# Strict load order, eight raw buffers and a held-back second half of batch 2, in a fused window-attention and mixture-of-experts kernel

The chip is one Trainium2, and the kernel runs on one of its cores. The metric is the device time of one execution in microseconds (us). Engines are named as in the profile: PE is TensorE (PEld its weight loads), DVE is VectorE, ACT is ScalarE, POOL is GpSimd, SP is SyncE. SPq, ACTq and POOLq are their instruction queues, where the issue of a DMA is recorded.

## The reference

```
B, H, S, D = 8, 8, 576, 64
scores = q @ k.T / sqrt(D), kept where |i - j| <= 32, softmax, then @ v
x      = heads side by side                            # (8, 576, 512)
e_idx  = argmax(x.mean(axis=1) @ w_gate)               # one expert per batch
out[b] = gate_w[b] * (relu(x[b] @ w1[e_idx[b]]) @ w2[e_idx[b]])
```

Each batch needs 2.36 MB of q and k in four loads, 1.18 MB of v, and 2.1 MB of fp16 weights of an expert that is known only when its attention is done. Each batch writes 1.18 MB in five stores.

## The kernel before

A small scheduler (the "plan") writes every operation into the in-order queues of the engines at build time. Three parts matter here. The plan gives each load a priority and a buffer:

```
buffers("raw", [P, 2, J, D], FP32, 5)        # q, k as loaded; batch 0 borrows weight space
vraws = buffers("vraw", ..., 2)
...
other = b == 1 and quad == 0                 # two loads of batch 1 go out by ScalarE
plan.add("ACT" if other else "SP", 0.6, f"ld{name}{b}{quad}", load,
         deps=["CT00k12_"] if other else [],
         takes=[("raw", 1)] if b else [], land=580e3, prio=-100 if other else base + quad)
```

A v load is a small tail (8 KB, first) and a bulk of 1.18 MB in rows of 256 bytes. Both go out by SyncE. The weights go out by GpSimd once the gate knows the expert. The last part is the output: ScalarE scales a PSUM tile into `osb` and then issues its store itself, from the same in-order queue:

```
nc.scalar.activation(osb[:, 0:w], bank..., ACTF.Copy, scale=gwb)      # "evac"
...
nc.scalar.dma_start(out[b, 128 * i : 128 * i + 128, :], osb)          # "store"
```

The softmax here doesn't subtract the row's maximum and nothing guards it: scores larger than these inputs give would overflow.

Of the kernel before, what the change touches and what calls it, by code (L numbers as in the profile page):

```python
# [10 lines left out]
FP32 = mybir.dt.float32  # L11
# [9 lines left out]
D = 64  # L21
# [4 lines left out]
P = 128  # L26
# [3 lines left out]
J = S // G  # L30
# [188 lines left out]
def kernel(  # L219
# [10 lines left out]
    nc = tc.nc  # L230
# [4 lines left out]
    plan = Plan()  # L235

    def buffers(name, shape, dtype, n):
        tiles = [sb.tile(shape, dtype, name=f"{name}{i}") for i in range(n)]
        plan.resource(name, tiles)
        return tiles  # L240


    rowi = sb.tile([P, 32], FP32, name="rowi")
    buffers("raw", [P, 2, J, D], FP32, 5)
    vraws = buffers("vraw", [P, NVS + 1, D], FP32, 2)
    w1s = buffers("w1", [P, NDT, F], FP16, 2)
    w2s = buffers("w2", [P, NFT, DM], FP16, 2)
# [1 line left out]
    roomy = [  # L249
        t.rearrange("p a c -> p (a c)").bitcast(FP32)[:, 0 : 2 * J * D]  # L250
        .rearrange("p (h j d) -> p h j d", h=2, j=J)
        for t in (w1s[0], w2s[0], w1s[1], w2s[1])
    ]
# [37 lines left out]
    zero = sb.tile([P, P], FP16, name="zero")  # L291
# [62 lines left out]
    def warm(op):  # L354
# [4 lines left out]
             deps=[f"CT11{n}" for n in ("q12", "k12")], prio=500)  # L359
# [7 lines left out]
    raw = {}  # L367
# [20 lines left out]
    def add_batch(b):  # L388
        base = b * 1000


        for quad in range(2):
            for name, src in (("q", q), ("k", k)):
                def load(op, b=b, quad=quad, name=name, src=src):
                    t = op.got["raw"][0] if b else roomy.pop(0)
                    raw[(b, quad, name)] = t
                    (nc.scalar if op.eng == "ACT" else nc.sync).dma_start(
                        t.rearrange("p h j d -> p h (j d)"),
                        src[b, 4 * quad : 4 * quad + 4]
                        .rearrange("(h x) s d -> (x s d) h", h=2)  # L400
                        .rearrange("(p r) h -> p h r", p=P),
                    )
                other = b == 1 and quad == 0
                plan.add("ACT" if other else "SP", 0.6, f"ld{name}{b}{quad}", load,
                         deps=["CT00k12_"] if other else [],
                         takes=[("raw", 1)] if b else [],
                         land=580e3, prio=-100 if other else base + quad)

                for part, (j0, j1) in enumerate(PARTS):
                    def cast(op, b=b, quad=quad, name=name, part=part, j0=j0, j1=j1):  # L410
                        if part == 0:
                            qkb_of[(b, quad, name)] = op.got["qkb"][0]
                        dst = qkb_of[(b, quad, name)][:, j0:j1]
                        src = raw[(b, quad, name)].rearrange("p h j d -> p j h d")[:, j0:j1]
                        if op.eng == "SW":
                            nc.gpsimd.tensor_copy(dst, src)  # L416
                        else:
                            nc.scalar.copy(dst, src)
                    cn = f"c{name}{b}{quad}"
                    plan.add("SW/ACT" if b < 2 else "SW",  # L420
                             {"SW": 0.68, "ACT": 0.66} if part == 0 else {"SW": 0.55, "ACT": 0.56},
                             f"{cn}{part}", cast,
                             deps=[f"ld{name}{b}{quad}"] + ([f"{cn}0_"] if part else [])
                             + (["W10_"] if b == 2 else [])
                             + (["vr010_"] if b == 1 and quad else []),
                             takes=[] if part else [("qkb", 1)],
                             frees=[(f"ld{name}{b}{quad}", "raw")] if part and b else [],
                             prio=base + quad, port=0.6)

        for half in range(2):  # L430
            def loadv(op, half=half):

                if half == 0:
                    vr_of[b] = op.got["vraw"][0]
                    if b == 0:
                        va_of[b] = op.got["vaug"][0]
                t = vr_of[b]
                rows = v.rearrange("b h s d -> (b h s) d")
                r0 = b * H * S - 32
                if half:  # L440
                    j0 = 0 if b else 1
                    nc.sync.dma_start(
                        t[:, j0:NVS],
                        rows[r0 + 128 * j0 : r0 + 128 * NVS].rearrange("(j p) d -> p j d", p=P),
                    )
                    return
                if b == 0:
                    nc.sync.dma_start(t[32:P, 0], rows[0:96])
                nc.sync.dma_start(t[0:32, NVS], rows[r0 + 128 * NVS : r0 + 128 * NVS + 32])
            plan.add("SP", 0.6 if half or b else 1.0, f"ldv{b}{half}", loadv,  # L450
                     takes=[] if half else [("vraw", 1)] if b else [("vraw", 1), ("vaug", 1)],
                     land=1.4e6 if half else 0.03e6, prio=base + 2 + half,
                     deps=["zero"] + ([f"ldv{b}0_"] if half else []))

            def vcast(op, half=half):
                if half == 0 and b:
                    va_of[b] = op.got["vaug"][0]
                for j0, j1 in ((19, 28), (28, NVS + 1)) if half else ((0, 9), (9, 19)):
                    dst, src = va_of[b][:, 0, j0:j1, 0:D], vr_of[b][:, j0:j1]
                    if op.eng == "SW":  # L460
                        nc.gpsimd.tensor_copy(dst, src)  # L461
                    else:
                        copy(op, dst, src)
            plan.add(BOTH if b == 1 else "DVE" if b == 0 and not half else "SW",
                     {"DVE": 1.0, "ACT": 1.3, "SW": 1.25}, f"vc{b}{half}", vcast,
                     deps=[f"ldv{b}1", f"ldv{b}0"]
                     + (["cc"] if b == 0 else [f"S{b}000_"] if b > 1 else ["G0_"])
                     + (["vr000_", "vr001_"] if b == 0 and half else [])
                     + ([f"vc{b}0_"] if half else []),
                     takes=[] if half or b == 0 else [("vaug", 1)],  # L470
                     frees=[(f"ldv{b}0", "vraw")] if half else [],
                     prio=base + (2 + half if b == 0 else 120), port=0.6)

            for up in range(2):
                def rot(op, half=half, up=up):

                    s = slice(18 * half, 18 * half + 18)
                    t = slice(18 * half + up, 18 * half + 18 + up)
                    va = va_of[b]
                    if up:  # L480
                        copy(op, va[64:P, 1, s, 0:D],
                             va[0:64, 0, t, 0:D] if b or not half else vr_of[0][0:64, t])
                    else:
                        nc.vector.tensor_copy(va[0:64, 1, s, 0:D], va[64:P, 0, t, 0:D])  # L484
                plan.add("ACT" if b == 0 and up and half else "DVE", 1.15 if b == 0 and up and half else 0.5,
                         f"vr{b}{half}{up}", rot,
                         deps=["ldv01", "ldv00", "cc"] + ["XS0111"] * half if b == 0 and up and half else [f"vc{b}{half}"],
                         prio=base + (4 + half if b == 0 else 120), port=0.5)


        for quad in range(2):
            for name in ("q", "k"):
                for part, (j0, j1) in enumerate(PARTS):
# [3 lines left out]
                    def tr(op, quad=quad, name=name, j0=j0, j1=j1, first=first, tn=tn):  # L497
# [5 lines left out]
                        for j in range(j0, j1):  # L503
# [4 lines left out]
                             deps=[f"c{name}{b}{quad}{part}"] + ([f"T{b}{quad}{name}0"] if part else [])  # L508
                             + (["ca"] if b == 0 else []),
                             takes=[("psA" if b > 1 else "psE", 1)] + ([(name + "T", 1)] if first else []),  # L510
                             frees=[] if first else [(f"c{name}{b}{quad}0", "qkb")],
                             prio=base + (40 if b else 3) * quad + (10 if b else 1) * part)

                    def tcopy(op, quad=quad, name=name, j0=j0, j1=j1, tn=tn):
                        pv = bank_of[tn].bitcast(BF16).rearrange("p (j c) -> p c j", c=P)
                        dst = qkT[(b, quad, name)]
                        if name == "k":
# [8 lines left out]
                             deps=[tn] + (["G0_"] if b == 1 and quad else []),  # L526
                             frees=[(tn, "psA" if b > 1 else "psE")],
                             prio=base + (40 if b else 3) * quad + (10 if b else 1) * part)
# [3 lines left out]
        for n in range(5):  # L532
            half, quad = n // 2, n % 2
# [43 lines left out]
            if b == 0:  # L577
# [3 lines left out]
                     deps=[f"CT{b}{a}{x}{p}2" for x in "qk" for p in range(2) for a in quads]  # L581
# [3 lines left out]
                     takes=[("psA", 2)] + ([] if n else [("E", 1)]),  # L585
                     frees=[(f"T{b}{a}{x}0", x + "T") for a in range(2) for x in "qk"]
# [376 lines left out]
```

## Time and profile before

| | before |
|---|---|
| time, median of 3 runs (range) | 227.77 us (227.43 to 230.16) |
| profiled execution | span 228.3 us, PE busy 92%, mean clock 0.983 |
| PE's one long stop | 4.01 us, for batch 0's first weight |
| PE idle between 46 and 221 us | 4.85 us (175.00 less 170.15 busy) |

The 40 slices of the page show the whole run at a glance. Each digit is the busy share of a slice of 5.7 us, in tenths:

```profile
PE   7989992999998999999988999699999999999980
PEclk9999999799999999999999999999999999999996
DMA  6999999799999999999999899989932993798041
```

The 2 in the PE row is the stop at 35 to 39 us, and the 7 below it is the clock that fell behind it. The DMA engines are full until about 160 us.

A second reading turned out to matter far more than that stop. ScalarE's timeline around the second large stop shows the issue of a store (start us, us, engine, line, operation, count; in brackets the idle time before it and its releaser):

```profile
65.78 1.39 ACT L868 ACTIVATE hT<-bank 128x288 f16<-128x288 f32 x3 [0.80 <-PE bank L850]
69.27 0.35 ACTq L923 DMA_DIRECT2D out_dram<-osb  x1
69.66 1.01 ACT L868 ACTIVATE hT<-bank 128x288 f16<-128x288 f32 x3 [2.50 <-PE bank L504]
```

Nothing runs on ScalarE from 67.2 to 69.27. Then the store is issued, and the next activation follows at once. ScalarE had stood at the store. PE lost 0.75 us by it.

### The profile page before, as it was taken

How to read it: one execution, taken by the hardware profiler on the slowest of the kernel's cores; microseconds unless marked ns; L12 is line 12 of the kernel's file. 1: busy time of each engine (PE TensorE's matmuls, PEld its weight loads, DVE VectorE, ACT ScalarE, POOL GpSimd, SP SyncE). 2: the span in 40 equal slices, each digit the busy share in tenths (PEclk: the TensorE clock that was granted, in tenths of full speed). 3: DMA queues.
4: the chain of work that ended last, by engine and by line, in shares of the span. 5: the costliest groups of instructions: out<-in, count | busy, mean ns of one | idle time of the engine just before them, and what ended most of it. 6: DMA issues, size and time to landing. Idle time of an engine off the chain costs nothing. (4 is left out here: it accounts for less than half of the span.)

```text
span 228.3 us, 6814 instructions
## 1 busy us (share of the span) xinstructions
PE 209.8 (92%) x2778; PEld 155.4 (68%) x2778; DVE 144.5 (63%) x369; ACT 148.5 (65%) x332; POOL 80.0 (35%) x126
## 2 busy tenths in 40 slices
PE   7989992999998999999988999699999999999980
PEld 5757762896488756986587758685598568749630
DVE  6478784156986897959866878569987676000000
ACT  4667981569657972898338955599289647647540
POOL 6436190008961193059033920459104100200000
PEclk9999999799999999999999999999999999999996
DMA  6999999799999999999999899989932993798041
GB/s 223 352 395 288 303 311 229 174 387 301 237 286 399 287 176 249 350 347 230 245 374 304 192 234 325 294 236 197 231 119 26 205 230 120 121 213 230 15 170 37
DMA packets 26639, 55.03 MB, mean 241 GB/s; under 512 B 2064, under 2 KB 12272, under 8 KB 24560
## 3 DMA queue, kind: packets, MB, share of 16 engines
q0 software_dynamic: 2304, 16.78, 38.0%
q1 hardware_dynamic: 18112, 27.21, 35.2%
q10 hardware_dynamic: 6192, 10.62, 12.4%
q8 instruction: 21, 0.34, 0.6%
q14 instruction: 10, 0.08, 0.1%
HBM read 61.94 MB, written 9.44 MB: 313 GB/s over the span
## 5 line engine op out<-in xcount | busy, mean ns | idle before, releaser
L850 PE MATMUL bank<-xT,w 128*128 128x288 f16 x512 | 75.0, 292 | 7.4 <-DMA w<-in_moe_w_dram 4.0
L850 PEld LDWEIGHTS <-w 128*128 128x128 f16 x512 | 61.6, 146 | 9.9 <-DMA w<-in_moe_w_dram 4.3
L868 ACT ACTIVATE hT<-bank 128x288 f16<-128x288 f32 x128 | 50.7, 424 | 16.7 <-PE bank L850 11.4
L886 PE MATMUL bank<-w,hT 128*128 128x512 f16 x256 | 60.5, 380 | 0.0
L416 POOL CAST qkb<-raw 128x640 bf16<-128x640 f32 (+1 forms) x54 | 42.7, 833 | 27.2 <-DMA raw<-in_q_dram 16.5
L912 ACT ACTIVATE osb<-bank,gwb 128x512 f32<-128x512 f32 (+1 forms) x40 | 25.8, 645 | 37.0 <-PE bank L886 33.0
L599 ACT ACTIVATE E<-bank 128x512 f16<-128x512 f32 (+1 forms) x80 | 41.7, 585 | 2.9 <-PE bank L557 2.8
L886 PEld LDWEIGHTS <-hT 128*128 128x128 f16 x256 | 23.1, 98 | 23.8
L820 POOL DMA_DIRECT2D w<-in_moe_w_dram x8 | 5.0, 630 | 83.2 <-DVE gw L812 47.3
L617 DVE TENSOR_TENSOR E<-E,mask 128x1024 f16<-128x1024 f16 (+1 forms) x30 | 25.7, 876 | 7.7 <-ACT E L599 7.5
L651 DVE TENSOR_TENSOR xs<-bank,linv 128x256 f16<-128x256 f32 (+2 forms) x88 | 27.6, 348 | 1.8
L504 PE MATMUL bank<-id_bf,qkb 128*128 128x128 bf16 x288 | 23.3, 219 | 1.2 <-ACT xT L386 1.2
L504 PEld LDWEIGHTS <-qkb 128*128 128x128 bf16 x288 | 18.7, 98 | 4.8 <-issue 1.3
L461 POOL CAST vaug<-vraw 128x576 f16<-128x576 f32 (+1 forms) x26 | 19.8, 815 | 0.0
L633 PEld LDWEIGHTS <-E 128*64 128x64 f16 x640 | 12.5, 111 | 8.2 <-issue 6.1
L386 ACT COPY xT<-bank 128x512 f16<-128x512 f16 (+1 forms) x24 | 12.3, 540 | 8.0 <-DVE kT L384 2.8
L633 PE MATMUL bank<-vaug,E 128*64 128x65 f16 x640 | 15.5, 197 | 1.8 <-DVE vaug L384 1.2
L557 PEld LDWEIGHTS <-kT 64*128 64x128 bf16 x576 | 10.7, 95 | 9.3 <-issue 7.7
L355 PE MATMUL bank<-wide,zero 128*128 128x256 f16 x94 | 15.5, 303 | 1.4 <-POOL wide L297 1.4
L557 PE MATMUL bank<-qT,kT 64*128 64x64 bf16 x576 | 15.4, 191 | 0.0
L384 DVE COPY xT<-bank 128x512 f16<-128x512 f16 (+1 forms) x16 | 6.4, 403 | 13.9 <-PE bank L711 13.8
L643 DVE RECIPROCAL linv<-bank 128x7 f32<-128x7 f32 (+2 forms) x56 | 10.5, 188 | 6.0 <-PE bank L633 5.9
(71 smaller groups left out, 200.2 us busy)
## 6 DMA issues: line engine op xcount, KB each, us to landing
w<-in_moe_w_dram POOLq DMA_DIRECT2D x16, 1024.0 KB, 13.0
out_dram<-osb ACTq DMA_DIRECT2D x32, 256.0 KB, 6.0
raw<-in_q_dram SPq DMA_DIRECT2D x13, 576.0 KB, 12.3
raw<-in_k_dram SPq DMA_DIRECT2D x13, 576.0 KB, 14.1
w<-in_q_dram SPq DMA_DIRECT2D x2, 576.0 KB
w<-in_k_dram SPq DMA_DIRECT2D x2, 576.0 KB, 7.6
out_dram<-osb ACTq DMA_DIRECT2D x8, 128.0 KB
raw<-in_q_dram ACTq DMA_DIRECT2D x1, 576.0 KB, 6.3
```

The source lines that it names most:

```text
L416: nc.gpsimd.tensor_copy(dst, src)
L461: nc.gpsimd.tensor_copy(dst, src)
L504: nc.tensor.transpose(pv[:, j - j0, :], qkb_of[(b, quad, name)][:, j], id_bf)
L557: nc.tensor.matmul(bank[:, 64 * place : 64 * place + 64], qkT[(b, a, "k")][rows, k0 : k0 + P], qkT[(b, a, "q")][rows, k0 : k0 + 64], start ...
L599: nc.scalar.activation(dst, src, ACTF.Exp, bias=0.0, scale=0.125)
L617: nc.vector.tensor_tensor(ev, ev, mv, ALU.mult)
L633: nc.tensor.matmul(bank[64 * n : 64 * n + 64, 65 * u : 65 * u + 65], E_of[b][:, h, 64 * block : 64 * block + 64], va_of[b][:, late, slot, ...
L651: nc.vector.tensor_tensor(xv[:, quad, hp : hp + u1 - u0], hv[0:n, u0:u1, 0:64], linv[0:n, u0:u1].to_broadcast([n, u1 - u0, 64]), ALU.mult,)
L850: nc.tensor.matmul(bank[:, 0:288], w_of[b][0].rearrange("p t (c n) -> p t n c", c=P)[:, dt, ft], xT_of[b][:, dt, 288 * c : 288 * c + 288], ...
L868: nc.scalar.activation(h_of[(b, ft)][:, 288 * c : 288 * c + 288], bank_of.pop(gn)[:, 0:288], ACTF.Relu,)
L886: nc.tensor.matmul(bank, h_of[(b, ft)][:, 128 * i : 128 * i + 128], w2s[:, ft, :], start=(ft == 0), stop=(ft == NFT - 1),)
L912: nc.scalar.activation(osb[:, 0:w], bank_of.pop(f"2{b}{i}")[:, 0:w], ACTF.Copy, bias=0.0, scale=tiny("gwb", [P, 1], FP32, b),)
```

## The change

The intent is to get batch 0's first weight sooner. The loads follow one strict order from SyncE alone. Eight raw buffers replace five, so that a load need not wait for a buffer. Batch 2's second q and k, its v and everything behind them wait for a one-column GpSimd write that stands behind the issue of batch 0's weights.

```
-    buffers("raw", [P, 2, J, D], FP32, 5)
+    buffers("raw", [P, 2, J, D], FP32, 8)
...
+                held = (b, quad, name) == (2, 1, "q")
+                def hold(op, b=b, quad=quad, name=name):
+                    t = raw[(b, quad, name)] = op.got["raw"][0]
+                    nc.gpsimd.memset(t[:, 0, 0, 0:1], 0.0)
+                if held:
+                    plan.add("SW", 0.1, "hold", hold, deps=["W20_"], takes=[("raw", 1)], prio=-5)
...
-                    (nc.scalar if op.eng == "ACT" else nc.sync).dma_start(
+                    nc.sync.dma_start(
...
-                other = b == 1 and quad == 0
-                plan.add("ACT" if other else "SP", 0.6, f"ld{name}{b}{quad}", load,
-                         deps=["CT00k12_"] if other else [],
+                plan.add("SP", 0.6, f"ld{name}{b}{quad}", load,
+                         deps=["hold"] * held + (
+                             ["ldv01_"] * (b == 1) if b < 2 else [f"ldq{b}{quad}_"] if name == "k"
+                             else [f"ldk{b}0_"] if quad else [f"ldv{b - 1}1_"] * (b > 2)),
+                         prio=1001.5 + 2 * quad if b == 2 else base + quad)
...
-                     deps=["zero"] + ([f"ldv{b}0_"] if half else []))
+                     deps=["zero"] + ([f"ldv{b}0_"] if half else ["ldk20_"] if b == 1
+                                      else [f"ldk{b}1_"] if b >= 2 else []))
```

(Cut: the held load takes the buffer that the hold took, the others take theirs as before; and the buffer's release is now by the hold's name where there is one.)

More of the change, by code (lines that the diff above doesn't have):

```diff
@@ L393, in add_batch, with load @@
             for name, src in (("q", q), ("k", k)):
-                def load(op, b=b, quad=quad, name=name, src=src):
-                    t = op.got["raw"][0] if b else roomy.pop(0)
-                    raw[(b, quad, name)] = t
-                    (nc.scalar if op.eng == "ACT" else nc.sync).dma_start(
+                held = (b, quad, name) == (2, 1, "q")
[4 more added lines that the diff above has]
+                    plan.add("SW", 0.1, "hold", hold, deps=["W20_"], takes=[("raw", 1)], prio=-5)
+                def load(op, b=b, quad=quad, name=name, src=src, held=held):
+                    if held:
+                        t = raw[(b, quad, name)]
+                    else:
+                        t = raw[(b, quad, name)] = op.got["raw"][0] if b else roomy.pop(0)
+                    nc.sync.dma_start(
                         t.rearrange("p h j d -> p h (j d)"),
@@ L402, in load @@
                     )
-                other = b == 1 and quad == 0
-                plan.add("ACT" if other else "SP", 0.6, f"ld{name}{b}{quad}", load,
-                         deps=["CT00k12_"] if other else [],
-                         takes=[("raw", 1)] if b else [],
-                         land=580e3, prio=-100 if other else base + quad)
+                plan.add("SP", 0.6, f"ld{name}{b}{quad}", load,
+                         takes=[("raw", 1)] if b and not held else [], land=580e3,
+                         deps=["hold"] * held + (
+                             ["ldv01_"] * (b == 1) if b < 2 else [f"ldq{b}{quad}_"] if name == "k"
+                             else [f"ldk{b}0_"] if quad else [f"ldv{b - 1}1_"] * (b > 2)),
+                         prio=1001.5 + 2 * quad if b == 2 else base + quad)
                 for part, (j0, j1) in enumerate(PARTS):
@@ L426, in add_batch @@
                              takes=[] if part else [("qkb", 1)],
-                             frees=[(f"ld{name}{b}{quad}", "raw")] if part and b else [],
+                             frees=[("hold" if held else f"ld{name}{b}{quad}", "raw")] if part and b else [],
                              prio=base + quad, port=0.6)
@@ L452, in add_batch @@
                      land=1.4e6 if half else 0.03e6, prio=base + 2 + half,
-                     deps=["zero"] + ([f"ldv{b}0_"] if half else []))
+                     deps=["zero"] + ([f"ldv{b}0_"] if half else ["ldk20_"] if b == 1 else [f"ldk{b}1_"] if b >= 2 else []))
             def vcast(op, half=half):
```

## The prediction

> **What bounds the kernel now.** I read the page first, then PE in order of time, then the stretches in which PE stood still, then the DMA queues microsecond by microsecond around the one long stop. From the page (engine, busy us, share of the span, instructions; then the costliest groups):
>
> ```profile
> span 228.3 us, 6814 instructions
> PE 209.8 (92%) x2778; PEld 155.4 (68%) x2778; DVE 144.5 (63%) x369; ACT 148.5 (65%) x332; POOL 80.0 (35%) x126
> L355 PE MATMUL bank<-wide,zero 128*128 128x256 f16 x94 | 15.5, 303 | 1.4 <-POOL wide L297 1.4
> ```
>
> PE is the bound, but 15.5 of its 209.8 us are the filler matmuls of L355, which end at 35 us. Real work is about 194 us. So the time is: when dense work starts, plus that work, plus a tail of 7 us of stores (221.3 to 228.3). Where dense work starts is seen in PE's timeline (start us, us, engine, line, operation, count, idle before and its releaser):
>
> ```profile
> 34.83 0.39 PE L355 MATMUL bank<-wide,zero 128*128 128x256 f16 x2
> 39.24 0.87 PE L850 MATMUL bank<-xT,w 128*128 128x288 f16 x4 [4.01 <-DMA w<-in_moe_w_dram]
> ```
>
> PE has done all that its order gives it by 35.1 and stands 4.0 us for batch 0's first expert weight (W1 of batch 0). It is PE's only long wait for a DMA. The windows around it (busy of PE, PEld, DVE, ACT, POOL; granted clock; DMA share; GB/s) show a second cost:
>
> ```profile
> 38.00:40.00 2.00, 0.76 (x5) 0.68 (x6) 0.00 (x0) 0.00 (x0) 0.00 (x0) 0.92 1.07 230
> 40.00:42.00 2.00, 2.00 (x12) 1.49 (x11) 0.00 (x0) 1.41 (x3) 0.00 (x0) 0.50 1.06 229
> 42.00:44.00 2.00, 2.00 (x16) 1.60 (x16) 0.42 (x1) 0.82 (x2) 0.00 (x0) 0.73 0.52 160
> ```
>
> After the stop the clock falls to 0.50. Over 39.24 to 46.0 the mean grant was 0.75 with PE busy throughout: 6.76 x 0.25 = 1.7 us lost. The stop thus costs 4.0 + 1.7 = 5.7 us. Why was the weight late? POOL's and SP's timelines:
>
> ```profile
> 27.47 0.69 POOL L820 DMA_DIRECT2D w<-in_moe_w_dram  x1 [6.16 <-DVE kT L384]
> 22.91 0.42 SPq L397 DMA_DIRECT2D raw<-in_q_dram  x1
> 23.43 0.41 SPq L397 DMA_DIRECT2D raw<-in_k_dram  x1
> 24.57 0.71 SPq L442 DMA_DIRECT2D vraw<-in_v_dram  x1
> 25.37 18.93 SPq L397 DMA_DIRECT2D raw<-in_q_dram  x1
> ```
>
> The weight is issued at 27.47, behind q, k (four times 0.59 MB) and v (1.18 MB) of batch 2, which SP issued from 21.8 to 25.3. The queue shares of 30 to 31, 31 to 32 and 33 to 34 us (queue: packets, MB, share of 16 engines), in that order:
>
> ```profile
> q1 hardware_dynamic: 310, 0.34, 101.6%
> ...
> q1 hardware_dynamic: 288, 0.29, 96.1%
> q0 software_dynamic: 8, 0.07, 31.2%
> ...
> q0 software_dynamic: 27, 0.22, 105.3%
> q1 hardware_dynamic: 26, 0.03, 9.6%
> ```
>
> q0 carries the weights, q1 SP's loads. Until 31.7 q1 has everything, 4.2 us after the issue. Then q0 has 90 to 105% and q1 about a tenth. A weight issued into a quiet queue does better. Landing of the first weight of batch 0, of batch 6 (issued 174.41) and of batch 7 (194.63), us in the last column:
>
> ```profile
> w<-in_moe_w_dram POOLq DMA_DIRECT2D x1, 1024.0 KB, 11.7
> ...
> w<-in_moe_w_dram POOLq DMA_DIRECT2D x1, 1024.0 KB, 8.5
> ...
> w<-in_moe_w_dram POOLq DMA_DIRECT2D x1, 1024.0 KB, 8.0
> ```
>
> For both late ones, q0's first packets appear 1.0 to 1.5 us after the issue. So 3 us of the 11.7 are the loads ahead of the weight, nearly all in its start.
>
> **What the Trainium skill says.** "DMA: Bandwidth & Descriptors", section "Queues, rings and completion order": each DMA engine goes round its queue rows one packet at a time. The trace agrees once the weight flows: 27 packets of q0 (8 KB each) beside 26 of q1 (1 KB, v) in that microsecond, so the big packets take nearly all the time. It doesn't tell why q0 first waited 4.2 us; here the measurement decides. Same page, "Issuing engines are not separate DMA queues": issuing from a second engine saves only issue time. It agrees: ACT issued batch 1's first q and k at 8.5 and 9.0, yet ACT's queue (q10) moved its first packets in 11 to 12 us, when v of batch 0 had drained. "TensorE: Matmul & The Clock Gate", "Part 1: The HAM clock gate": an idle window of about 3.4 us halves the PE clock. It agrees: 4.0 us idle, then 0.50.
>
> **The change, part by part.**
>
> Hold. One write of 0.1 us on POOL (the one-column memset L340 took 0.10), placed behind the issue of batch 0's second weight (28.7 now), ahead of batch 2's second q, k, its v and all later loads. 2 x 0.59 + 1.18 = 2.4 MB leave the queue that the weight meets. SP would issue them from about 28.9, first packets some 1.3 us later (q of batch 0: issued 0.84, packets from 2), after the weight has begun. Beside weights, q, k loads got 12 to 17% of the engines (58 to 62 us, 105 to 110 us). Five microseconds of that add about 0.7 us to 8.3: landing 9.0 us after issue.
>
> Order and buffers. Batch 1's first q, k move from ACT to SP. Since q10 moved nothing before 12 anyway, they lose little: SP gets past v of batch 0 at 11.7 now and issues at once, packets from about 13, so they land about 0.7 us later. ACT is freed of two issues (0.46 + 0.48 us), beside other work. Batch 2's first q, k go ahead of batch 1's v, which needs the sixth raw buffer; eight give the rest. Is the queue empty when the weight comes? Before, q, k, v of batches 0 and 1 (7.1 MB) had moved by 21.6. Now 1.18 MB more at 0.38 MB/us (3.1 us) and a hole of 1.0 us behind batch 0's v (like the one at 21.7 to 22.7 now, where SP got past a v load) give 25.7. That is 1.5 us ahead of the weight's issue, and ahead of batch 1's v cast (26.6 now).
>
> Gate of batch 0. Its v lost a few packets at 12 to 14 us beside q10, and DVE waited 0.75 us for it at 14.26. Alone in its queue it may land up to 0.75 earlier. As PE and DVE also wait for other things there, I take 0.3: weight issued 27.2.
>
> Sum. Weight lands 27.2 + 9.0 = 36.2 instead of 39.24: 3.0 us. PE is ready at 34.8, so a stop of 1.4 us is left, too short for the clock to fall: 1.7 us. Together 4.7 us.
>
> Downstream. From 39 to 221 PE idles only some 5 us. The main three are at 69, 119 and 145 us (0.75, 1.2, 1.7), each where ACT's in-order queue stood at the issue of an output store while loads crawled beside weights. At 69 it is plain: a q load issued at 47.3 took 21.9 us, to 69.2, and the store went at 69.27. More buffers bring some loads ahead of the weights, so fewer should crawl; a different order moves such waits about. I count 0.3 us of gain. All: 4.7 + 0.3 = 5.0, so 227.8 - 5.0 = 222.8 us.
>
> **Rivals.** (a) The hold comes too late to matter or the queue is still full: if v of batch 1 isn't through by 27.2, its 1 KB packets either delay the weight's start again or crawl at a tenth beside it, and batch 1's attention is late. For it: my drain time has only 1.5 us to spare. Against: 4 us of slack in batch 1's work, and fillers beside it. Time then 225 to 227. (b) The early gain is given back: DMA engines are nearly fully busy from 46 to 160 us (0.95 to 1.07), and held loads start 4 us later. With PE 5 us ahead, batch 3's second q, k would crawl beside batch 1's weights and land near 61. Against: from their casts (56 to 64 now) to their transposes (72 now) there's room, and before the change SP itself waited 30 us in all for raw buffers, so loads were paced by buffers, not by the engines. Given back 1 to 3 us: 224 to 226. (c) It is better than I say: the weight lands as PE runs out, and the three store waits go too: 2 to 3 us more, 220 to 221. (d) The q, k of batch 1, later by 0.7, hold up batch 0's gate in the in-order queues of POOL and PE: 1 us worse. PE takes batch 1's first transposes at 17.4, two us after those loads would land, so I hold it weak.
>
> **Range and chances.** The stop and its clock loss are the sure part. (a), (b) and (d) pull up, (c) down: 220.3 to 226.3. 2% is 4.6 us, so faster by over 2% means under 223.2, close to my centre: 0.55. Within 2%: 0.42. Slower: 0.03.
>
> **What would show it.** q1 quiet by 26 to 27 us, first q0 packets within 1.6 us of the issue; the weight landing 8.5 to 9.5 us after its issue; PE's stop at L850 under 2 us and the clock 1.00 from 36 to 46; q and k of batch 2's second half issued just behind the second weight. I'm wrong if the stop stays above 3 us, if the clock still falls, or if PE's idle after 46 us grows from 5 to over 7 us.

## The result, and the profile after

The changed kernel is slower: 239.59 us median of 4 runs (236.44 to 241.46) against 228.59 us of the kernel before on the same chip (4 runs, 227.43 to 230.16). The ratio is 1.0431, with a 95% interval of 1.0297 to 1.0565. All ratios here are the mean time of one kernel's fast runs over the mean of the other's fast runs of the same rounds, so they are not quite the ratio of the quoted medians. The outputs are correct.

The page of the kernel after, with the rows that answer to those of before:

```profile
span 237.7 us, 6842 instructions
...
PE 212.2 (89%) x2786; PEld 156.6 (66%) x2786; DVE 142.2 (60%) x367; ACT 151.3 (64%) x336; POOL 78.0 (33%) x125
...
PE   7999989999879892769798999998799999999980
PEclk9999999999999996599999999999999999999997
...
L862 PE MATMUL bank<-xT,w 128*128 128x288 f16 x512 | 76.4, 294 | 10.9 <-ACT osb L924 6.2
```

The 2 at slice 7 has gone, and with it the low clock at slice 8. A new hole stands at slices 16 to 18, with a clock of 0.6 and 0.5 in slices 16 and 17. The costliest group, the first expert product, now waits most for an eviction of ScalarE (`osb`), 6.2 us, where it waited 4.0 us for a weight.

**The front did what it was meant to.** First GpSimd's, then PE's timeline at the front:

```profile
25.99 0.69 POOL L832 DMA_DIRECT2D w<-in_moe_w_dram  x1 [3.78 <-DVE sexp L823]
...
34.82 1.20 PE L862 MATMUL bank<-xT,w 128*128 128x288 f16 x8 [0.96 <-DMA w<-in_moe_w_dram]
```

The weight is issued 1.48 us earlier than before and lands 8.8 us after its issue instead of 11.7. PE waits 0.96 us for it instead of 4.01. The window of 42 to 44 us, where the clock had been 0.73 before, shows no fall (busy of PE, PEld, DVE, ACT and POOL; clock; DMA share; GB/s):

```profile
42.00:44.00 2.00, 2.00 (x43) 1.89 (x42) 0.45 (x2) 1.05 (x4) 1.95 (x4) 1.00 1.11 343
```

**All of it, and 9 us more, is lost between the ends of batch 0 and batch 2.** A milestone for each batch makes that plain: when PE starts the last group of its second expert product (the 16 matmuls of L892 before, L904 after).

| batch | 0 | 1 | 2 | 3 | 4 | 5 | 6 | 7 |
|---|---|---|---|---|---|---|---|---|
| before, us | 63.40 | 90.12 | 113.57 | 138.94 | 164.68 | 187.65 | 204.59 | 220.48 |
| after, us | 57.33 | 87.47 | 123.33 | 148.14 | 173.78 | 196.96 | 213.90 | 229.79 |
| after less before | -6.1 | -2.7 | +9.8 | +9.2 | +9.1 | +9.3 | +9.3 | +9.3 |

From batch 2 on nothing changes any more. Of the loss, 3.4 us fall between the first two milestones: PE waited there for a weight (1.10 us, at 60), for ScalarE's copy of a transposed q (1.44 us, at 68) and for a cast (0.65 us, at 79). ScalarE was late with that copy because it stood some 2 us, up to 66.58, at a store of batch 0 whose tile had been ready since 58.1. The other two waits weren't followed further. The other 12.5 us fall between the second and the third. The windows of before, then of after, in that stretch:

```profile
90.00:100.00 10.00, 10.00 (x141) 8.98 (x141) 7.99 (x22) 8.14 (x20) 0.60 (x2) 1.00 1.03 339
```

```profile
90.00:100.00 10.00, 4.96 (x30) 3.86 (x30) 0.52 (x2) 2.04 (x4) 0.00 (x0) 0.55 0.95 337
...
80.00:110.00 30.00, 21.82 (x277) 15.70 (x276) 15.59 (x41) 12.31 (x28) 5.02 (x7) 0.83 0.99 302
```

PE did 30 matmuls in 10 us where it had done 141, with the clock at 0.55. From 80 to 110 us it was idle 8.2 of 30 us. ScalarE's timeline, then PE's, show what stood:

```profile
82.12 0.69 ACT L924 ACTIVATE osb<-bank,gwb 128x512 f32<-128x512 f32 x1
92.68 0.37 ACTq L935 DMA_DIRECT2D out_dram<-osb  x1
93.09 0.69 ACT L924 ACTIVATE osb<-bank,gwb 128x512 f32<-128x512 f32 x1 [10.29 <-DMA vraw<-in_v_dram]
...
101.69 0.59 ACT L386 COPY xT<-bank 128x512 f16<-128x512 f16 x1 [4.05 <-DMA vraw<-in_v_dram]
...
93.83 1.12 PE L862 MATMUL bank<-xT,w 128*128 128x288 f16 x4 [4.95 <-ACT osb L924]
```

ScalarE finished an eviction at 82.81 and stood 10 us at the issue of its store, until a v load had landed. At a later store it stood 4.05 us more. From 88.9 us PE had no work but what waited for that eviction. It stood 4.95 us, then 1.21 and 1.73 us. The store has nothing to do with v. It moves `osb` to the output.

Why was v so slow? SyncE's and GpSimd's timelines show the two issues side by side, and the third fence has the queue shares of one microsecond in between, 82 to 83 us (packets, MB, share of 16 engines):

```profile
74.52 0.71 SPq L454 DMA_DIRECT2D vraw<-in_v_dram  x1
76.03 14.86 SPq L408 DMA_DIRECT2D raw<-in_q_dram  x1
```

```profile
74.94 0.67 POOL L832 DMA_DIRECT2D w<-in_moe_w_dram  x1 [2.77 <-DVE gw L824]
```

```profile
q0 software_dynamic: 21, 0.17, 81.9%
q1 hardware_dynamic: 22, 0.02, 8.1%
```

v of batch 4 left 0.4 us ahead of batch 2's weights. In that microsecond 21 packets of weights moved beside 22 of v, but the weight packets are eight times as large (0.17 and 0.02 MB). That is the round by packets which the prediction cites. v got through at about 92, when the weights were done (from 91 to 92 us their queue moved nothing).

**Why the store waits for v.** The trace shows the wait. Its reason is seen in the compiled program, in the list of waits that each DMA carries. All DMAs of SyncE and ScalarE share eight completion semaphores, dealt round in program order, and each DMA waits for the one that had its semaphore before it. A program order for the kernel after (O = output store of batch and tile, v4 = bulk, v4t = tail; GpSimd's DMAs left out):

```
... q40 k40 O02 q41 O03 k41 O04 v4t v4  q50 k50 q51 k51 v5t v5  O10 O11 q60 O12 ...
O11, the second store of batch 1, has the semaphore of v4, eight places ahead
O13, which stood 4.05 us at 101 us, has that of v5t
before: ... O10 has O02's semaphore, O11 q50's, O12 k50's, O13 q51's, O14 O10's
```

With eight raw buffers and this order, all of batch 5's loads stand ahead of batch 1's stores in the program, so the first two stores of batch 1 pair with v4t and v4. The kernel before had such pairs too: by its program, batch 0's fourth store (O03) has the semaphore of batch 4's first q, and that is the store at 69.27 us shown above. The Trainium skill says in "DMA: Bandwidth & Descriptors", section "Why a DMA increments its semaphore by 16 and not by 1", that two DMAs in flight on one semaphore can fool a wait, so the wait is not idle caution. The same page, section "Anatomy of one DMA — SWDGE (gpsimd) path", says that the DMA engines don't wait on semaphores and that a wait is served by the issuing sequencer. The trace agrees: it is ScalarE that stood, 10.29 us.

### The profile page after: what moved, and what is told of

It is laid out like the page before. It is cut to its first block, busy times and chain, and to the rows that moved or that the text cites. A ratio compares the mean times of both kernels' runs of the same rounds, so it can differ in the third digit from the quotient of the medians.

```text
span 237.7 us, 6842 instructions
## 1 busy us (share of the span) xinstructions
PE 212.2 (89%) x2786; PEld 156.6 (66%) x2786; DVE 142.2 (60%) x367; ACT 151.3 (64%) x336; POOL 78.0 (33%) x125
## 4 chain that ended last, share of the span: by engine, by line
PE 55%; DMA 18%; DVE 9%; SPq 4%; POOL 4%; ACT 3%; issue 2%; POOLq 0%; ACTq 0%; DVEq 0%
PE bank L862 19%; PE bank L898 15%; DMA raw<-in_k_dram 11%; PE bank L516 5%; SPq L408 4%; DMA w<-in_moe_w_dram 4%; PE bank L355 4%; DMA vraw<-in_v_dram 4%; PE bank L645 3%; DVE E L629 3%; PE bank L723 3%; POOL qkb L428 3%; PE bank L569 2%; PE bank L904 2%; DVE vaug L496 2%
## 5 line engine op out<-in xcount | busy, mean ns | idle before, releaser
L862 PE MATMUL bank<-xT,w 128*128 128x288 f16 x512 | 76.4, 294 | 10.9 <-ACT osb L924 6.2
L898 PE MATMUL bank<-w,hT 128*128 128x512 f16 x256 | 59.7, 380 | 0.0
L428 POOL CAST qkb<-raw 128x512 bf16<-128x512 f32 (+1 forms) x53 | 42.9, 855 | 24.1 <-DMA raw<-in_q_dram 11.1
L645 PEld LDWEIGHTS <-E 128*64 128x64 f16 x640 | 12.6, 111 | 10.7 <-issue 4.9
L386 ACT COPY qT<-bank 128x640 bf16<-128x640 bf16 (+1 forms) x20 | 14.6, 756 | 5.8 <-PE bank L516 3.2
L355 PE MATMUL bank<-wide,zero 128*128 128x256 f16 x102 | 16.1, 302 | 1.4 <-POOL wide L297 1.4
L384 DVE COPY xT<-bank 128x512 f16<-128x512 f16 (+1 forms) x21 | 8.1, 396 | 15.0 <-PE bank L723 14.7
L775 DVE TENSOR_REDUCE pooled<-xT 128x4 f32<-128x1536 f16 x6 | 10.5, 1749 | 8.4 <-ACT xT L386 8.4
L386 ACT COPY xT<-bank 128x512 f16<-128x512 f16 (+1 forms) x19 | 10.0, 547 | 8.4 <-DMA vraw<-in_v_dram 4.1
## 6 DMA issues: line engine op xcount, KB each, us to landing
w<-in_moe_w_dram POOLq DMA_DIRECT2D x16, 1024.0 KB, 12.6
```

Source lines behind the costliest of these rows:

```text
L355: nc.tensor.matmul(banks[7][:, 0:256], zero, wide, start=True, stop=True, skip_group_check=True)
L386: nc.scalar.copy(dst, src)
L428: nc.gpsimd.tensor_copy(dst, src)
L645: nc.tensor.matmul(bank[64 * n : 64 * n + 64, 65 * u : 65 * u + 65], E_of[b][:, h, 64 * block : 64 * block + 64], va_of[b][:, late, slot, ...
L862: nc.tensor.matmul(bank[:, 0:288], w_of[b][0].rearrange("p t (c n) -> p t n c", c=P)[:, dt, ft], xT_of[b][:, dt, 288 * c : 288 * c + 288], ...
L898: nc.tensor.matmul(bank, h_of[(b, ft)][:, 128 * i : 128 * i + 128], w2s[:, ft, :], start=(ft == 0), stop=(ft == NFT - 1),)
```

## The experiments

Sixteen kernels ran in five lots, each beside the kernel before on its own chip. Beside a few changed lines, each compiled to another program order, so I read the semaphore pairs of each from its compiled program before it ran. On one core "slow" only means more than 1.5% above the kernel's fastest run. For a kernel whose runs scatter widely this flatters the ratio: 12 of the 20 runs of late are left out by it, against 6 of 23 of the kernel before. By the 2% rule nohold, buf5, before8, late_nohold, vpool_stores, late_vpool and v3_scalar are slower than before, v2_scalar_late is unclear, and all the others are the same.

| run | what it is | median us (runs) | before us, same chip | ratio, 95% interval |
|---|---|---|---|---|
| late | after, loads of batches 5 to 7 behind stores | 228.82 (20) | 229.29 | 0.9899 (0.9860 to 0.9937) |
| nohold | after without the hold | 244.73 (4) | 229.29 | 1.0664 (1.0565 to 1.0763) |
| buf5 | after with five buffers | 239.75 (4) | 229.29 | 1.0453 (1.0379 to 1.0528) |
| before8 | before with eight buffers | 235.72 (4) | 229.29 | 1.0301 (1.0209 to 1.0394) |
| poolstores | after, stores by GpSimd | 231.12 (4) | 229.02 | 1.0137 (1.0084 to 1.0189) |
| before_ps | before, stores by GpSimd | 228.78 (20) | 229.02 | 0.9978 (0.9948 to 1.0009) |
| late_nohold | late without the hold | 234.33 (4) | 229.02 | 1.0254 (1.0205 to 1.0303) |
| poolstores_late | both | 230.93 (4) | 229.02 | 1.0110 (1.0064 to 1.0157) |
| vpool_stores | poolstores, v by GpSimd | 243.13 (4) | 229.16 | 1.0589 (1.0495 to 1.0683) |
| vact_stores | poolstores, v of 1 to 7 by ScalarE | 230.71 (20) | 229.16 | 1.0071 (1.0049 to 1.0094) |
| late_vpool | late, v by GpSimd | 247.66 (4) | 229.16 | 1.0803 (1.0733 to 1.0872) |
| before_vpool | before_ps, v by GpSimd | wrong output | | |
| v3_scalar | poolstores, v of 3 to 7 by ScalarE | 239.46 (4) | 228.99 | 1.0433 (1.0360 to 1.0507) |
| v2_scalar | poolstores, v of 2 to 7 by ScalarE | 228.82 (12) | 228.99 | 0.9980 (0.9951 to 1.0009) |
| v3_scalar_before | before_ps, v of 3 to 7 by ScalarE | 226.91 (4) | 228.99 | 0.9886 (0.9815 to 0.9957) |
| v2_scalar_late | v2_scalar, v of 3 later | 232.43 (4) | 228.55 | 1.0169 (1.0096 to 1.0242) |

Theory A was the one above: ScalarE stands at a store whose semaphore still belongs to a load that crawls beside weights. The rival, B, was that the strict order simply starves a batch of its loads. A third, C, was that eight buffers let loads run ahead and take the DMA engines from the weights.

### late: keep the loads of batch b + 4 behind the stores of batch b

```
+ late = b in (5, 6, 7) and (quad, name) == (0, "q")
+ def tiny_write(op): nc.scalar.copy(t[:, 0, 0, 0:1], zero[:, 0:1])      # into the raw buffer
+ plan.add("ACT", 0.2, f"late{b}", tiny_write, deps=[f"O{b - 4}4_"], takes=[("raw", 1)])
```

> The changed kernel; the first q load of batches 5, 6 and 7 now also waits for a one-column write by ACT placed behind the last output store of batch 1, 2 and 3. Nothing else is altered, but the completion semaphores (eight, dealt out in the order of the program over all loads and stores of SP and ACT) fall otherwise: the second store of batch 1 shares its semaphore with the third store of batch 0 and no longer with v of batch 4. Theory A (the store waits at the head of ACT's queue for a v load that crawls beside weights): ACT's stop of 10 us at 82.8 us is gone, PE's stops of 5.0, 1.2 and 1.7 us after 88 us and the low clock with them: 224 to 230 us. Rival B (the loss is that held and ordered loads bring batch 3's and 4's data late): no change, 236 us or more. Rival C (eight buffers let loads run ahead and take the DMA engines from the weights): little change, 235 or more, as batch 4's loads run as early as before.

The result was 228.82 us, 10.8 us under the changed kernel (medians of different chips), and a ratio of 0.9899 to before. The front stays:

```profile
34.00 1.20 PE L870 MATMUL bank<-xT,w 128*128 128x288 f16 x8 [0.67 <-DMA w<-in_moe_w_dram]
```

The 10 us stop is gone. The largest stop of PE after 60 us is 1.59 us, at 165 us. The profiled execution was one of the slow ones of this kernel, so I take from it only which stops are there. Nothing of the changed kernel's loads was taken away here. Their place in the program against the stores was changed, and by that also when they leave. Theory A's forecast came true, and those of B (236 us or more) and C (235 or more) did not. Whether late is better than before isn't shown: the 1.0% of the ratio comes from the eight runs called fast, and with all runs counted the means are 228.50 and 229.18 us, 0.3% apart.

### nohold, buf5, before8: one part of the change at a time

nohold sets `held = False`; buf5 puts 5 in place of 8; before8 puts 8 in place of 5 in the kernel before.

> The changed kernel without the hold: batch 2's second q, k, its v and all behind are issued as soon as buffers and semaphores allow; every engine's order is the same. The early gain should go: the first weight lands 11 to 12 us after its issue, PE stops 3 to 4 us at its first expert matmul and the clock falls. Theory A: v of batch 3 is through before batch 1's weights are issued, and the second store of batch 1 shares a semaphore with the last store of batch 0, so no long stop of ACT at 83 us: 227 to 233 us. Rival B (held loads are the cause): 227 to 231. Rival C (buffers and order): 236 or more.

> The changed kernel with five raw buffers in place of eight; the planned order of every engine is unchanged. In the program the first two stores of batch 1 now share semaphores with stores of batch 0, the third and fourth with the first q and k of batch 5. But k of batch 2 must wait for a buffer, so v of batch 1 is later and can meet the first weight. Theory A: ACT's stop moves from the second store to the third of batch 1 and is shorter (3 to 6 us in place of 10), some loss in front: 229 to 236. Rival B: as the changed kernel or worse, 238 or more, since loads come later still. Rival C: 227 to 230.

> The kernel before with eight raw buffers and nothing else of the change. Its plan is made anew, so orders differ. Theory A: the first stop (4 us) stays or grows, since batch 2's loads are issued even earlier; stores of batch 1 share semaphores with the tail and the bulk of v of batch 5 (the third and fourth store), so a stop of ACT is possible there: 228 to 240. Rival B: no slower than before, 225 to 229. Rival C: slower, 233 or more.

All three are slower than before, each by a stop of the same kind at another store. First nohold's timelines of SyncE, ScalarE and PE:

```profile
18.43 9.12 SPq L408 DMA_DIRECT2D raw<-in_q_dram  x1
...
72.51 0.41 ACT L880 ACTIVATE hT<-bank 128x288 f16<-128x288 f32 x1 [10.08 <-DMA raw<-in_q_dram]
...
72.97 0.88 PE L862 MATMUL bank<-xT,w 128*128 128x288 f16 x3 [8.33 <-ACT hT L880]
```

Then buf5's ScalarE:

```profile
96.68 1.05 ACT L924 ACTIVATE osb<-bank,gwb 128x512 f32<-128x512 f32 x2 [12.24 <-DMA raw<-in_q_dram]
```

nohold missed my range by 12 us upwards, for I hadn't looked at all its pairs: batch 0's third store shares a semaphore with batch 4's first q. A second stop of ScalarE, 7.42 us at 107 us behind a v load, came on top. It also shows that the hold does little. SyncE stood 9.12 us at batch 2's second q anyway, behind v of batch 1, until 27.55, so the weight (issued 26.76) met a nearly quiet queue without any hold, and PE waited for it only until 36.12. That keeps 3.1 of the 4.4 us by which the changed kernel starts sooner (39.24 to 34.82). buf5 keeps 4.1 of them (35.12), and before8, with eight buffers alone, has a wait of 3.78 us until 38.69. So most of the front's gain comes from the order; no run has the order without both the hold and the eight buffers. buf5's stop moved to the store that I had named (the third of batch 1), but was 12.24 us long where I expected 3 to 6, and the time is 3.8 us over my range. By the time alone, rival B (238 or more) fits buf5, and rival C (236 and 233 or more) fits nohold and before8. What speaks for A in them is the trace: each stop stands at a store, and the load that the trace names as its releaser is the store's partner in the program. Five buffers with the new order are no cure. before8 shows the other half: eight buffers alone cost the old order 3.0%, by a stop of 5.10 us and one of 3.18 us behind v loads.

### poolstores and before_ps: take the stores off ScalarE

```
- nc.scalar.dma_start(out[b, 128 * i : 128 * i + 128, :], osb)
+ nc.gpsimd.dma_start(out[b, 128 * i : 128 * i + 128, :], osb)      # other semaphores, weights' queue
```

> The kernel after, with its output stores issued by GpSimd instead of ScalarE, so that no store shares a completion semaphore with a load of q, k or v. The loads, their order, the eight buffers and the hold are untouched. Theory A (the loss is ScalarE standing at a store whose semaphore still belongs to a bulk v or a q load that crawls beside the weights): no stop of ScalarE above 1 us whose releaser is a load and which stands behind a store; the 10.3 us stop at 93 us and TensorE's 4.95 us stop behind it are gone, the clock over 90 to 100 us stays above 0.95, and the time is 222 to 229 us. Theory B (the strict order starves a batch of its own loads, whatever the stores do): TensorE still stops for several us between 85 and 110 us, with casts or transposes as releasers, and the time stays above 234 us. A risk on the side: GpSimd's own queue of weights may now stand at a store, which would show as weights issued later.

> The kernel before with the same edit of the stores. It keeps the 4.0 us stop for batch 0's first weight at 39 us, and loses its own three stops of ScalarE at stores (67, 117 and 143 us, behind which TensorE stood 0.75, 1.2 and 1.7 us): 224 to 229 us. Against the run of the kernel after with the same edit it gives what the change is worth where semaphores are out of the way: theory A says that one is 0 to 4 us faster than this one, theory B that it is slower by over 5 us.

No store of poolstores stands behind a load, and it is 8.5 us faster than the changed kernel. That is theory A again, by another route. But it is 2 us over the range, and 2.3 us slower than the control, where theory A wanted it 0 to 4 us faster and theory B over 5 us slower. So neither theory alone is enough. It is slower although its milestones lead the control's by 6.0 us at batch 0 and 6.5 at batch 1 (57.81 and 81.72 against 63.81 and 88.24). At batch 2 they are 0.4 us behind (111.45 against 111.07), and 2.1 us at the end. So there is a second cost, smaller than the first. poolstores in SyncE's and in PE's timeline:

```profile
72.74 22.32 SPq L406 DMA_DIRECT2D raw<-in_q_dram  x1
```

```profile
91.00 0.71 PE L514 MATMUL bank<-id_bf,qkb 128*128 128x128 bf16 x5 [1.77 <-POOL qkb L426]
```

SyncE stands at the load behind each bulk v until that v is nearly through (14.26, 21.83, 22.32 and 20.39 us). The changed kernel has such stands too (14.13, 20.87 and 14.86 us). So batch 4's other q and k left at 69.65 to 71 us, with batch 2's weights (69.42), and were cast at 86.7 to 93 us. PE waited for the casts, and the clock was 0.50 from 92 to 96 us. This is a form of theory B, so the rival was partly right.

### late_nohold and poolstores_late: the two cures combined

> The run late (a small ScalarE write ahead of the first q load of batches 5, 6 and 7, behind the last store of batches 1, 2 and 3) without the hold of batch 2's second half. The run without hold and without late lost 17 us to two stops of ScalarE at stores and none at the front. Here the pairs of stores and loads differ again: the third store of batch 0 follows batch 4's first q, the second store of batch 1 batch 4's second q, the fourth and fifth the v of batch 4. Theory A: the third store of batch 0 stands again about 10 us at 72 us, as it did without hold, since late touches only batches 5 to 7; time 236 to 244 us. If the hold itself were harmful, this would be faster than late's 228.8.

> The kernel after with both: output stores from GpSimd, and the small ScalarE write that holds the first q load of batches 5, 6 and 7 until the last store of batches 1, 2 and 3 is issued. If the late write helped only by changing which load a store is paired with (theory A), it adds nothing here: within 1.5 us of the run with the stores alone moved. If it helped because it keeps loads from crawling beside weights and taking their place, it is faster than that run by over 2 us.

late_nohold came out at 234.33 us with the stop at the third store of batch 0 that was expected (10.13 us on ScalarE, 8.39 us on PE at 72.25). It was 1.7 us below the range. poolstores_late is within 0.2 us of poolstores. The tiny write adds nothing once stores and loads share no semaphore, which speaks for the pairing, not the later start of the loads, as what it mended in late.

### v in another queue: vpool_stores, vact_stores, late_vpool, before_vpool

```
- nc.sync.dma_start(t[:, j0:NVS], rows[...])                     # bulk of v
+ (nc.gpsimd if b else nc.sync).dma_start(t[:, j0:NVS], rows[...])    # or nc.scalar, with the stores on GpSimd
```

> The kernel after with stores issued by GpSimd (as in the run poolstores) and the bulk of v of batches 1 to 7 issued by GpSimd as well, on the weights' queue. In poolstores SyncE stood 14.3, 21.8, 22.3 and 20.4 us at the q load behind each bulk v, so batch 4's q and k left at 69.7 to 71 us, beside batch 2's weights (69.4 us), and were cast at 86.7 to 93 us: TensorE stopped 1.77 us at 91 us and its clock was 0.50 over 92 to 96 us. Theory B2 (this standing behind v is what is left of the loss): no stop of SyncE over 8 us at a q load after 45 us, no stop of TensorE over 1 us between 60 and 110 us, clock above 0.95 there, and 221 to 227 us. Theory C (q and k loads would crawl beside weights however early they are issued, or GpSimd's time for issuing v eats the gain): 228 us or more, with casts of q and k still late. The v issue on GpSimd may take several us; that is watched.

> As vpool_stores, but with the bulk of v issued by ScalarE, which issues nothing else here (the stores go by GpSimd). It parts two ways of getting v out of SyncE's queue: here v still is slow beside the weights, but q and k need not stand behind it. Theory B2: the same as vpool_stores within 2 us, 221 to 227 us. If v's own landing counts (the values are cast just before a batch's attention), this is slower than vpool_stores, with a wait for v of over 2 us at ScalarE, DVE or GpSimd.

> The run late (stores on ScalarE, first q load of batches 5 to 7 held until the last store of batches 1 to 3) with the bulk of v issued by GpSimd. In late two small losses are left at 139 us (ScalarE 2.49 us behind a q load; TensorE 1.42 us) and at 162 to 165 us. With v out of SyncE's queue the loads land sooner and the stores' partners are done: no stop of ScalarE over 1.5 us with a load as releaser, 222 to 227 us under theory B2; under theory C 228 us or more.

> The kernel before with both edits of vpool_stores (stores and the bulk of v from GpSimd). It says what the change is worth where no store stands behind a load and no q or k behind a v. The front keeps before's stop of about 4 us for batch 0's first weight, unless v in the weights' queue shortens it: 223 to 229 us. The step of the prediction that gave the front 3 us and the clock 1.7 us says that vpool_stores is 3 to 6 us faster than this.

v on GpSimd is bad. vpool_stores and late_vpool miss their ranges by 16 and 21 us. One v issue took GpSimd 1.84 to 1.89 us, and in vpool_stores it was busy 25.70 of 30 us from 60 to 90 us (15.73 in poolstores), with batch 2's weights issued only at 96.60. SyncE's 20 us stops were gone, so that half of the expectation held, but the path moved to GpSimd. before_vpool gave a wrong output (relative error 0.053), although the check for races before the run found nothing. I didn't find the reason and use no time of it. vact_stores is 3.7 us over its range. In it PE was busy 149.0 of 150 us between 60 and 210 us, which is what I had hoped for, but ScalarE stood 7.26 us at 51 us at v of batch 3, which had been given the semaphore of v of batch 2, and PE stood 6.83 us behind it: the first mechanism once more, now between two loads.

### v3_scalar, v2_scalar, v3_scalar_before, v2_scalar_late: is the early front worth anything?

These take that stop away by leaving v of batch 2 (or only of batch 1) with SyncE, or by moving v of batch 3.

> As vact_stores, but only v of batches 3 to 7 is issued by ScalarE; v of batches 1 and 2 stays with SyncE as in the kernel after. In vact_stores TensorE was busy 22.26 of 30 us between 30 and 60 us (ScalarE stood 7.26 us at the issue of v of batch 3, which waited for v of batch 2), and 149.0 of 150 us between 60 and 210 us. Here v of batch 2 has been through since about 44 us, so that stop goes. If SyncE standing behind v is what was left of the loss: no stop of TensorE over 1.5 us after 37 us, and 222 to 226 us. If loads are slow beside weights anyway: stops of over 1.5 us at casts or transposes between 60 and 120 us, and 228 us or more.

> The same with v of batches 2 to 7 on ScalarE. v of batch 3 now shares its semaphore with a q load of batch 3, which is issued ahead of v of batch 2, so ScalarE should not stand at it for over 1 us. What differs from v3_scalar is that q and k of batch 3 may run beside v of batch 2 from 30 us on: 222 to 227 us, within 2 us of v3_scalar. If v of batch 2 comes so late that batch 2 waits for it (it took 18.3 us from 32.7 us in vact_stores), this is slower by over 2 us.

> The control: the kernel before with both edits of v3_scalar. The stop of about 3.5 us for batch 0's first weight at 39 us stays; behind it the same flow of loads as in v3_scalar. If the change is worth its front and nothing else once semaphores and SyncE's queue are out of the way, v3_scalar is 3 to 6 us faster than this; this at 226 to 230 us.

> As v2_scalar, with the bulk of v of batch 3 put behind the cast of batch 3's first q, so that the load whose semaphore it shares (or a later one) is through by then and ScalarE need not stand. If that stop was what cost the front its gain: no stop of ScalarE over 1.5 us at a v issue, PE busy 29 of 30 us between 30 and 60 us, clock above 0.95 there, and 221 to 226 us, faster than v3_scalar_before's 226.9. If v of batch 3 then comes too late for batch 3's attention, TensorE stops for several us at about 75 to 90 us with v as the releaser, as in v3_scalar (10.94 us), and the time is over 230 us.

v3_scalar missed by 13 us, and is 12.6 us slower than its control where 3 to 6 us faster was expected: v of batch 3, issued at 54.98 us, was through only at 89, and PE stood for its cast. ScalarE stood 12.04 us at v of batch 4, which has the semaphore of that v.

```profile
89.68 0.21 PE L643 MATMUL bank<-vaug,E 128*64 128x65 f16 x1 [10.94 <-POOL vaug L471]
```

v2_scalar ended 1.8 us above its range. From 60 us on its PE stands still only once for over 1 us (1.15 us at 116 us). Its loss is early. ScalarE's and PE's timelines:

```profile
46.98 0.02 ACT L452 MOVE_SHAPE vraw<-in_v_dram  x1 [3.79 <-DMA raw<-in_q_dram]
...
48.65 1.65 PE L514 MATMUL bank<-id_bf,qkb 128*128 128x128 bf16 x14 [3.38 <-ACT qT L384]
```

Again a DMA issued by ScalarE waited for a load (by the program, batch 3's first q), where I had expected less than 1 us. The clock was 0.76 from 46 to 60 us, which makes 14 x 0.24 = 3.4 us, with the idle time partly in it. The lead of 6 us was gone at batch 0's milestone (64.46 us, against 63.67 in the control v3_scalar_before). v2_scalar_late should have freed it. Up to 60 us it did: PE was busy 28.93 of 30 us from 30 to 60, with the clock at 1.00, and reached batch 0's milestone at 59.44 us. But the other order paired v of batch 3 with batch 3's last k, and ScalarE stood 5.43 us at 62 us (PE 2.17 us behind it). My expectation that the shared load would be through was wrong. The longer stop came next, from the second cost: ScalarE stood in the issue of v of batch 4, right behind v of batch 3, as SyncE does elsewhere. ScalarE's and PE's timelines:

```profile
67.38 7.89 ACTq L452 DMA_DIRECT2D vraw<-in_v_dram  x1
...
75.73 0.69 PE L514 MATMUL bank<-id_bf,qkb 128*128 128x128 bf16 x5 [4.89 <-ACT xT L384]
```

The best version of all is v3_scalar_before at 226.91 us, ratio 0.9886. It is the old order with five buffers, with the stores on GpSimd and v of batches 3 to 7 on ScalarE. It is faster than both kernels (in its own lot 2.1 us under before, which is within the 2%). No version with the early front had a median below 228.8 us.

## Why the prediction was wrong

By its own steps:

1. **Hold, order, gate, landing.** The weight was predicted to be issued at 27.2 and to land 9.0 us later, and it was issued at 25.99 and landed after 8.8. The stop left was 0.96 us, not 1.4. The clock stayed at 1.00, as predicted. At batch 0's milestone the gain was 6.1 us where 4.7 were predicted, mostly because the gate came 1.48 us sooner where 0.3 was taken; why it did wasn't looked into. The mechanism was right. Only the credit to the hold was too large: nohold kept 3.1 of the 4.4 us.
2. **Downstream. This step failed.** It said "I count 0.3 us of gain." The milestones show a loss of 6.1 + 9.3 = 15.4 us, all of it between batch 0's and batch 2's. PE idled 16.1 us between 46 and 230 us (184.00 less 167.94), over the 7 us that the prediction gave as its own sign of being wrong.
3. **What stood in its place.** I had seen the three stops at stores and written "More buffers bring some loads ahead of the weights, so fewer should crawl; a different order moves such waits about." At 69 us I had even named the q load that held the store up, and rightly. But I took such waits for small ones and didn't ask why that store waits for that load, so I couldn't tell what the new program would pair. The eight buffers and the order put batch 5's loads ahead of batch 1's stores in the program, so a store came to share its semaphore with v of batch 4, which took some 18 us beside the weights. ScalarE stood 10.29 us at that store and PE 4.95 us behind it. late, which changes the pairing (and delays the loads of batches 5 to 7), and poolstores, which changes the issuing engine, win back 10.8 and 8.5 us.
4. **Rival (b)** named "held loads" that crawl beside weights and gave it 224 to 226. poolstores shows it as the second, smaller cost, though for batch 4's loads and not batch 3's: a lead of 6.5 us lost within a batch. The argument against it, that there was room between cast and transpose, did not hold at 86 to 93 us.
5. **The chance of slower, 0.03,** followed from treating the downstream waits as small. Nothing in the profile of before bounded them: each was already a stop of the engine that evicts PSUM, with a length set by an unrelated transfer.

**What stays open.** What all of the 3.4 us before the second milestone of the changed kernel come from. Why poolstores loses another 2.4 us in batch 3 after the loss in batch 2, and whether an order exists in which the early front is kept to the end. Each order that I tried put a load or a store behind another slow one. A semaphore of its own for every DMA wasn't tried, since the program's semaphores are dealt by the framework. The wrong output of before_vpool is unexplained.

## What to carry to other kernels

A store issued from an engine that also evicts PSUM is a possible stop of PE, so before you move loads or add buffers, list for each store and load which earlier DMA it shares a completion semaphore with, and how long that one flies. A slow neighbour on the DMA engines (small rows beside large weight packets) did little harm here until something on the path waited for it. And when an early gain is won, follow a milestone for each batch to the end: here it showed in one line that the gain was there and where it was lost.

## What the Trainium skill lacked or had wrong

- "DMA: Bandwidth & Descriptors" says where a wait is served and why a semaphore shouldn't be shared by DMAs in flight, but no page says that a program may deal a few semaphores over all loads and stores, so that a store waits for an unrelated load. Here that was a stop of 10.29 us, and of 12.24, 10.08 and 5.10 us in three other kernels.
- The same page gives the round by packets, but not what it does to a load of 256-byte rows: v took 8.1% of the engines beside weights with 81.9%, and some 18 us to land (74.5 to 92.6).
- No page says that the issuing engine stands at the load behind such a v until v is nearly through: SyncE 14.26 to 22.32 us in poolstores and 9.12 us in nohold, ScalarE 7.89 us in v2_scalar_late.
- The same page doesn't tell that a weight issued by GpSimd starts late behind a full SyncE queue: 4.2 us after its issue in the kernel before, 1.0 to 1.5 us in a quiet one.
- No page gives what it costs GpSimd to issue a bulk v (36 rows on each of 128 partitions): 1.84 to 1.89 us, against 0.55 us for a store.
- "TensorE: Matmul & The Clock Gate", section "Part 1: The HAM clock gate", ties the half clock to an idle window of about 3.4 us. Stops of 4.01 us (0.50 after it) and 0.96 us (no fall) agree. But in poolstores the clock fell to 0.50 in a stop of only 1.77 us, before 91.0 us, while a stop of 1.72 us at 146 us in the kernel before left it at 1.00. So the length of a stop alone didn't decide it here.
